# A hand-planned instruction order, computed again with longer transfer prices

## The chip, the cores and the metric

The kernel runs on one core of one Trainium2 chip. The metric is the device time of one execution in microseconds (us); the median of three runs is given, and one further execution was recorded by the profiler.

## The reference

Three layers follow one another. The first is a gated linear recurrence for 4 sequences, 8 heads, 768 steps and heads of 48: per step a complex decay, normalised to at most 0.999 in magnitude, multiplies the 48 x 48 state, the outer product of k and v is added, and q reads the real part. The result is a matrix of 3072 tokens by 384 columns. Two feed-forward layers (384 to 2048 to 384) follow, the first with a leaky ReLU, the second with an ELU:

```
for t in range(S):
    new_re = ar * S_re - ai * S_im
    new_im = ar * S_im + ai * S_re
    S_re, S_im = new_re + k_t v_t^T, new_im
    y[t] = q_t @ S_re
x = reshape(y);  h = x @ w_in;  x = max(0.01 * h, h) @ w_out
h = x @ w_in2;   out = where(h > 0, h, exp(min(h, 0)) - 1) @ w_out2
```

## The kernel before, in words

**Attention.** The 3072 tokens are 24 tiles (6 chunks of 128 steps by 4 sequences). For each tile ScalarE (ACT) and VectorE (DVE) compute decays and phases, scale k and q, and write two halves of `st` (L473, 128 x 768 floats each, cosine and sine part). Each half goes to a scratch tensor in HBM (L480) and is read back with other partitions as `f` (L482); `st` has one buffer. TensorE (PE) transposes `st` (L497), multiplies `f` by `f` (L510) into scores, DVE masks them (`am`, L515), PE multiplies by `v` and by the carried state (L530, L535), and L559 makes the state's increment. The result leaves PSUM in two float16 parts: ACT writes `xh` (L543), and DVE writes the rest, `xl` (L544). Four small moves per tile (L548, two for `xh`, two for `xl`, 12 KB each) then carry rows to other partitions of the same tile.

**Feed-forward.** Three tiles make a block of 384 tokens; there are 8 blocks per layer. A block goes over 16 weight slices: nine hidden matmuls (L596), an activation on ACT and DVE (L604 to L613), and two steps later nine matmuls into accumulators (L632). The blocks' order is written by hand: 1, 1, 2, 1, 2, 1, 2, ... (the layer's number). Weights are loaded as 64-bit words (L326, L329, two raw buffers) and converted to float16 pairs by DVE and ACT (L347 to L359), each slice once before its first use; checks of weights and inputs (L338, L340, L382 and others) fill ACT.

**The planner.** The program doesn't issue these in the order of the code. Every operation is an entry with an engine, a price in ns and its dependences; a transfer is two entries, 475 ns on SP (which issues all transfers, in order) and its own price on one server called DMA, which takes one transfer at a time. `HOPS` gives the delay from one engine's end to another's start: SP to DMA 650, DMA to SP 900. A list scheduler goes forward and backward over the graph for 11 rounds and keeps the order with the earliest end. The engines then run their instructions in that fixed order; real waits are semaphores, so the prices change the order and nothing else, with one exception. Where the plan shows PE idle for more than 700 ns, `(gap - 300) / 220` filler matmuls on the identity are put in (L750, each two records in the trace).

One dependence is known to the program but not to the planner: L544 reads 112 partitions of `xh`, among them rows that the moves of `xh` write. Where a move of `xh` is issued ahead of L544 in the order, L544 waits for it.

Of the kernel before, what the change touches and what calls it, by code (L numbers as in the profile page):

```python
# [124 lines left out]
class Plan:  # L125
# [5 lines left out]
    HOPS = {("DVE", "ACT"): 200.0, ("PE", "ACT"): 200.0, ("PE", "DVE"): 200.0, ("DVE", "PE"): 270.0,  # L131
            ("ACT", "PE"): 270.0, ("PE", "PE"): 0.0, ("ACT", "POOL"): 270.0, ("DVE", "POOL"): 160.0,
            ("DVE", "SP"): 120.0, ("PE", "SP"): 190.0, ("SP", "DMA"): 650.0, ("DMA", "SP"): 900.0,
            ("DMA", "DVE"): 907.0, ("DMA", "ACT"): 908.0, ("DMA", "PE"): 1067.0, ("DMA", "POOL"): 983.0}
    SWITCH = 1300.0
    ISSUE = 475.0
    ROUNDS = 11
# [131 lines left out]
def fast_path(ctx, tc, aa, kq, vt, w_in1, w_out1, w_in2, w_out2, st_dram, out):  # L269
    nc = tc.nc  # L270
# [24 lines left out]
    plan = Plan(lambda table: nc.scalar.preload_act_table_set(sets[table]))  # L295
# [102 lines left out]
    def attention(i):  # L398
# [55 lines left out]
        def scan_t():  # L454
            for j in range(KJ):
# [6 lines left out]
                r=[ph], w=[nf])  # L462
# [14 lines left out]
        scr = st_dram[i % 2]  # L477
        dr = plan.buf(None, None, None, "scr", 2)
        for cs in range(2):
            plan.op("SP", 1150, lambda cs=cs: nc.sync.dma_start(  # L480
                scr[cs].rearrange("(p j) w -> p j w", j=KJ), st.t[:, cs]), r=[st.part(cs)], w=[dr.part(cs)])
            plan.op("SP", 1900, lambda cs=cs: nc.sync.dma_start(  # L482
                f.t[D * cs:D * (cs + 1)], scr[cs].rearrange("(h d) w -> d h w", d=D)), r=[dr.part(cs)], w=[f.part(cs)])
        fp = [f.part(0), f.part(1)]

# [4 lines left out]
        if not last:  # L490
            kn = plan.buf(cp, [P, H, 2, DE, KJ], F32, "kn", KN_BUFS)
            for cs in range(2):
                pt = pa()

                def tr(cs=cs, pt=pt):
# [6 lines left out]
                    r=[pt], w=[kn.part(cs)])  # L502
        am = []
        for g in range(2):
            pt = pa()

            def sc(g=g, pt=pt):
# [9 lines left out]
                r=[pt], w=[m])  # L517
# [27 lines left out]
            xl.t[:wide, :, span], py4(), SX, xh.t[:wide, :, span], ALU.mult, ALU.subtract), r=[py, xh], w=[xl])  # L545
        for z, xz in enumerate((xh, xl)):
            for r in range(2):
                plan.op("SP", 200, lambda xz=xz, r=r: nc.sync.dma_start(  # L548
                    xz.t[64 * r + D:64 * (r + 1), 0:KJ, span],
                    xz.t[64 * r:64 * r + D, KJ, span]),  # L550
                    r=[xz], w=[x1[k][z].part((q, r))])
        parts = [xh, x1[k][0].part((q, 0)), x1[k][0].part((q, 1))]
        squares(parts, lambda: xh.t[:, 0:KJ, span], N, lambda: flags.t[:, 2, i:i + 1], flags.part((2, i)))
        if not last:
# [11 lines left out]
            else:  # L566
                plan.op("DVE", dve(N), lambda: V.tensor_tensor(state[b].t, pk3(), state[b].t, ALU.add),
                        r=[pk], w=[state[b]])
            if c % 2:
# [7 lines left out]
                    r=[rows], w=[pe])  # L577
                plan.op("DVE", dve(N), lambda: V.tensor_tensor(
                    state[b].t, state[b].t, pe.t[:2 * D, :H].unsqueeze(2).to_broadcast([2 * D, H, D]), ALU.mult),
                    r=[pe], w=[state[b]])  # L580
# [86 lines left out]


    running = {i: attention(i) for i in range(NT)}

    def attend(k):
# [267 lines left out]
```

## Time and profile before

| | before |
|---|---|
| median of 3 runs | 997.23 us (995.08 to 998.86) |
| the profiled execution | 991.79 us, of it a span of 990.0 us |
| PE busy | 931.8 us (94%), 6441 matmul records |
| ACT busy, DVE busy | 700.4 us (71%), 677.9 us (68%) |
| transfers | 121.92 MB, 41.1% of 16 engines' span on the SP queue |

PE's records overlap, so its busy share says only where it had something in flight. A window's clock is the mean granted TensorE clock as a share of 2.4 GHz; 0.50 is the lower level, 1.2 GHz. The chain of work that ended last is followed back from the last instruction.

### The profile page before, as it was taken

The numbers are of one execution on the slowest core, as the hardware profiler recorded it, in microseconds if no ns is written. First come the engines' busy times: TensorE is split into PE (matmuls) and PEld (weight loads), VectorE is DVE, ScalarE is ACT, GpSimd is POOL, SyncE is SP. The second block draws the span as 40 slices with busy tenths as digits, with TensorE's granted clock in tenths as the row PEclk, the third lists the DMA queues.
The fourth block names the chain that finished last, engine by engine and source line by source line (L and its number), as shares of the span: only waits on it lengthen the run. The fifth ranks groups of instructions, "written<-read, shape, count | busy, mean of one in ns | idle before, by whom it ended". The sixth has DMA issues, their size and how long they took to land.

```text
span 990.0 us, 17096 instructions
## 1 busy us (share of the span) xinstructions
PE 931.8 (94%) x6441; PEld 616.9 (62%) x6441; DVE 677.9 (68%) x1328; ACT 700.4 (71%) x1526; POOL 1.5 (0%) x21
## 2 busy tenths in 40 slices
PE   4498989999899899999989999999999999999997
PEld 4496666566666657666656667666665666666664
DVE  7878989999786568755677558855587554445553
ACT  6756578676599899999989756875578654345553
POOL 0000000000000000000000000000000000000000
PEclk8697999999899999999999999999999999999999
DMA  7783683664536636935668003620146002000000
GB/s 246 227 241 122 212 230 119 189 201 148 154 118 196 168 99 193 280 116 157 198 163 239 29 11 98 180 63 1 44 116 208 25 1 55 25 1 1 13 13 28
DMA packets 86747, 121.92 MB, mean 123 GB/s; under 512 B 11904, under 2 KB 69248, under 8 KB 86656
## 3 DMA queue, kind: packets, MB, share of 16 engines
q1 hardware_dynamic: 86656, 120.75, 41.1%
q8 instruction: 52, 0.85, 0.4%
q14 instruction: 39, 0.32, 0.1%
HBM read 95.94 MB, written 23.59 MB: 121 GB/s over the span
## 4 chain that ended last, share of the span: by engine, by line
PE 52%; ACT 19%; DVE 16%; DMA 9%; issue 3%; SPq 1%; DVEq 0%; ACTq 0%
PE acc L632 22%; PE h L596 22%; ACT wr L340 3%; DMA wr<-in_w_in 3%; PE pa L510 2%; ACT gh L612 2%; DMA xh<-xh 2%; DMA f<-stack_scratch 2%; DVE st L473 2%; DVE w L359 2%; ACT wt L338 2%; PE h L750 2%; DVE wt L349 2%; DVE g L609 1%; DVE wr L352 1%
## 5 line engine op out<-in xcount | busy, mean ns | idle before, releaser
L596 PEld LDWEIGHTS <-w 128*128 128x128 f16 x2304 | 225.2, 98 | 151.7 <-issue 8.5
L613 DVE TENSOR_TENSOR gl<-g,gh 128x384 f16<-128x384 f32 x256 | 141.5, 553 | 88.7 <-ACT gh L612 84.9
L612 ACT ACTIVATE gh<-g 128x384 f16<-128x384 f32 x256 | 133.2, 521 | 90.9 <-DVE g L609 88.4
L632 PE MATMUL acc<-w,gh 128*128 128x384 f16 x768 | 189.1, 329 | 0.0
L632 PE MATMUL acc<-gh,w 128*128 128x384 f16 x768 | 187.3, 326 | 0.3 <-ACT o L664 0.3
L609 DVE SCALAR_TENSOR_TENSOR g<-h,g 128x384 f32<-128x384 f32 x256 | 141.5, 553 | 54.9 <-ACT g L604 51.0
L632 PEld LDWEIGHTS <-w 128*128 128x128 f16 x1152 | 112.5, 98 | 75.1 <-issue 2.0
L596 PE MATMUL h<-yh,w 128*128 128x384 f16 x768 | 146.5, 327 | 3.2 <-DVE g L609 3.2
L596 PE MATMUL h<-xh,w 128*128 128x384 f16 x768 | 145.7, 326 | 0.5 <-DVE g L609 0.2
L632 PE MATMUL acc<-w,gl 128*128 128x384 f16 x384 | 126.0, 328 | 2.3 <-DVE gl L613 2.3
L632 PE MATMUL acc<-gl,w 128*128 128x384 f16 x384 | 125.2, 326 | 1.4 <-DVE gl L613 1.3
L632 PEld LDWEIGHTS <-gh 128*128 128x128 f16 x768 | 75.0, 99 | 48.7 <-issue 2.3
L608 DVE TENSOR_SCALAR g<-g 128x384 f32<-128x384 f32 x128 | 45.5, 356 | 77.8 <-ACT g L607 77.5
L606 ACT ACTIVATE g<-h 128x384 f32<-128x384 f32 x128 | 62.2, 486 | 49.5 <-PE h L596 47.4
L604 ACT ACTIVATE g<-h 128x384 f32<-128x384 f32 x128 | 62.0, 484 | 32.8 <-PE h L596 32.4
L596 PE MATMUL h<-xl,w 128*128 128x384 f16 x384 | 83.3, 326 | 0.0
L596 PE MATMUL h<-yl,w 128*128 128x384 f16 x384 | 83.3, 326 | 0.0
L607 ACT ACTIVATE g<-g 128x384 f32<-128x384 f32 x128 | 66.6, 521 | 2.4
L340 ACT ACTIVATE wr<-wt,consts 128x768 f32<-128x768 f32 x64 | 64.3, 1005 | 0.4
L632 PEld LDWEIGHTS <-gl 128*128 128x128 f16 x384 | 37.8, 98 | 29.0 <-DVE gl L613 3.9
L510 PE MATMUL pa<-f 96*128 96x128 f32 x384 | 49.7, 282 | 6.3 <-DMA f<-stack_scratch 3.4
L510 PEld LDWEIGHTS pa<-f 96*128 96x128 f32 x384 | 47.8, 197 | 9.2 <-issue 3.3
(99 smaller groups left out, 1121.8 us busy)
## 6 DMA issues: line engine op xcount, KB each, us to landing
wr<-in_w_out SPq DMA_DIRECT2D x64, 384.0 KB, 3.5
wr<-in_w_in SPq DMA_DIRECT2D x64, 384.0 KB, 4.1
stack_scratch<-st SPq DMA_DIRECT2D x48, 384.0 KB, 3.9
f<-stack_scratch SPq DMA_DIRECT2D x48, 384.0 KB, 5.6
kq<-in_kq SPq DMA_DIRECT2D x24, 384.0 KB, 4.8
re<-in_aa SPq DMA_DIRECT2D x32, 192.0 KB, 2.4
im<-in_aa SPq DMA_DIRECT2D x32, 192.0 KB, 2.7
v<-in_v SPq DMA_DIRECT2D x24, 192.0 KB, 3.4
```

The lines of the kernel that those rows point to most:

```text
L338: plan.op("ACT", act(2 * DM), lambda: S_.activation(t.t, raw.t[:, :, :, 1].bitcast(F32), AF.Abs), r=both, w=[t])
L340: plan.op("ACT", act(2 * DM) + 2 * EXTRA, lambda side=side, scale=scale, bias=bias: S_.activation(raw.t[:, :, :, 0].bitcast(F32), t.t, AF. ...
L510: T_.matmul(pt.t[:, hh * C:(hh + 1) * C], lhsT=f.t[:, h, 0:C], rhs=f.t[:, h, C:2 * C], start=True, stop=True)
L596: T_.matmul(ph.t[:, :n], lhsT=w.t[:, 0, z, j * P:(j + 1) * P], rhs=x.t[:, j, :n], start=(m == 0), stop=(m == len(seq) - 1))
L604: plan.op("ACT", act(n, True), lambda: S_.activation(g.t[:, :n], ph.t[:, :n], AF.Copy, scale=0.01 * c), r=[ph], w=[g])
L606: plan.op("ACT", act(n, True), lambda: S_.activation(g.t[:, :n], ph.t[:, :n], AF.Relu, scale=-1.0 / (SX * SW)), r=[ph], w=[g])
L607: plan.op("ACT", act(n), lambda: S_.activation(g.t[:, :n], g.t[:, :n], AF.Exp, scale=-1.0), w=[g], table="L")
L608: plan.op("DVE", dve(n, True), lambda: V.tensor_scalar(g.t[:, :n], g.t[:, :n], -1.0, SG, ALU.add, ALU.mult), w=[g])
L609: plan.op("DVE", dve(n), lambda: V.scalar_tensor_tensor(g.t[:, :n], ph.t[:, :n], c, g.t[:, :n], ALU.mult, ALU.max), r=[ph], w=[g])
L612: plan.op("ACT", act(n), lambda: S_.activation(gh.t[:, :n], g.t[:, :n], AF.Copy), r=[g], w=[gh])
L613: plan.op("DVE", dve(n), lambda: V.tensor_tensor(gl.t[:, :n], g.t[:, :n], gh.t[:, :n], ALU.subtract), r=[g, gh], w=[gl])
L632: T_.matmul(acc[o].t[:, :width], lhsT=pair[0], rhs=pair[1], start=(f == 0 and m == 0), stop=(f == KF - 1 and m == 2))
```

## The change

Eight prices of the planner are raised. No instruction of the program is added, taken away or altered apart from the fillers, whose number follows the plan's gaps.

```diff
-            ("DMA", "DVE"): 907.0, ("DMA", "ACT"): 908.0, ("DMA", "PE"): 1067.0, ("DMA", "POOL"): 983.0}
+            ("DMA", "DVE"): 1400.0, ("DMA", "ACT"): 1400.0, ("DMA", "PE"): 1800.0, ("DMA", "POOL"): 983.0}
...
         for cs in range(2):
-            plan.op("SP", 1150, lambda cs=cs: nc.sync.dma_start(
+            plan.op("SP", 1500, lambda cs=cs: nc.sync.dma_start(
                 scr[cs].rearrange("(p j) w -> p j w", j=KJ), st.t[:, cs]), r=[st.part(cs)], w=[dr.part(cs)])
-            plan.op("SP", 1900, lambda cs=cs: nc.sync.dma_start(
+            plan.op("SP", 2350, lambda cs=cs: nc.sync.dma_start(
                 f.t[D * cs:D * (cs + 1)], scr[cs].rearrange("(h d) w -> d h w", d=D)), r=[dr.part(cs)], w=[f.part(cs)])
...
             for r in range(2):
-                plan.op("SP", 200, lambda xz=xz, r=r: nc.sync.dma_start(
+                plan.op("SP", 600, lambda xz=xz, r=r: nc.sync.dma_start(
                     xz.t[64 * r + D:64 * (r + 1), 0:KJ, span],
```

## Rows read from the trace of the kernel before

**Rows 1.** Windows by stage: us, each engine's busy time, clock, transfer share, GB/s

```profile
0.00:100.00 100.00, 66.44 (x504) 60.75 (x505) 82.34 (x150) 63.73 (x123) 1.54 (x21) 0.81 0.69 210
100.00:250.00 150.00, 144.96 (x1015) 94.39 (x1013) 143.05 (x260) 103.22 (x216) 0.00 (x0) 1.00 0.63 186
250.00:520.00 270.00, 257.89 (x1814) 168.84 (x1814) 181.88 (x375) 246.67 (x550) 0.00 (x0) 0.98 0.56 166
520.00:960.00 440.00, 439.75 (x2975) 279.41 (x2974) 260.42 (x526) 276.33 (x619) 0.00 (x0) 1.00 0.22 63
```

**Rows 2.** Chain of work that ended last, late part: start, us, what

```profile
565.43 1.79 PE pa L510 x16
...
868.60 1.46 PE h L596 x9
...
917.84 2.44 PE acc L632 x15
```

**Rows 3.** The same chain of work, first 92 us

```profile
39.10 9.59 PE h L750 x66
...
66.21 5.67 DMA xh<-xh
...
83.42 6.33 PE h L750 x36
89.75 1.48 PE h L596 x9
```

**Rows 4.** Timeline of SP, 65 to 67 us

```profile
65.73 0.43 SPq L326 DMA_DIRECT2D wr<-in_w_in  x1
```

**Rows 5.** Timeline of PE, 77 us: in brackets idle before, and its releaser

```profile
77.86 1.12 PE L530 MATMUL pa<-am,v 128*64 128x128 f32 x8 [4.68 <-DVE am L515]
```

**Rows 6.** Waits of DVE: us in total, times, longest

```profile
DVE xl L544 <- DMA xh<-xh: 21.3, 9, 5.3
```

**Rows 7.** The chain of work, 254 to 266 us

```profile
254.85 3.72 DMA xh<-xh
...
259.41 2.08 PE pa L510 x8
...
262.45 1.71 PE pa L510 x8
264.16 2.19 PE h L596 x9
```

**Rows 8.** Waits of PE: us in total, times, longest

```profile
PE pa L510 <- DMA f<-stack_scratch: 3.4, 4, 2.6
...
PE pa L510 <- DVE xl L544: 2.0, 1, 2.0
```

**Rows 9.** The chain of work, 487 to 509 us

```profile
487.17 5.00 DMA stack_scratch<-st
493.69 8.71 DMA f<-stack_scratch
...
502.54 2.03 PE pa L510 x16
504.57 4.11 PE acc L632 x15
```

**Rows 10.** Windows of three short stretches, columns as in the first group

```profile
75.00:89.60 14.60, 11.13 (x69) 10.39 (x70) 13.19 (x25) 8.74 (x19) 0.00 (x0) 0.65 0.44 132
261.00:264.20 3.20, 3.20 (x15) 2.64 (x14) 2.37 (x5) 1.52 (x4) 0.00 (x0) 0.50 0.04 9
502.50:507.20 4.70, 4.66 (x25) 3.21 (x26) 2.95 (x7) 3.56 (x9) 0.00 (x0) 0.71 0.45 147
```

**Rows 11.** Transfer issues: KB each, median us from issue to landing

```profile
stack_scratch<-st SPq DMA_DIRECT2D x48, 384.0 KB, 3.9
f<-stack_scratch SPq DMA_DIRECT2D x48, 384.0 KB, 5.6
...
xh<-xh SPq DMA_DIRECT2D x48, 12.0 KB, 1.8
```

## The prediction

> **What bounds the kernel now.** I read the windows by stage first, then the chain of work, then who waits for whom. From 520 to 960 us PE is never idle for more than a quarter of a microsecond, at full clock [rows 1]: no order of the same instructions makes this part shorter. From 100 to 250 us PE is idle for 150 - 144.96 = 5.0 us while DVE is full, and from 250 to 520 us for 270 - 257.89 = 12.1 us while ACT is 91% busy [rows 1]. Ahead of that, the first hidden matmul starts at about 89.6 us [rows 3], and 16 us of the chain before it are filler [rows 3]. So the time is a start-up of some 90 us, then a PE that has work nearly always, then a short tail. An order can win or lose only (a) when the first hidden matmul starts and (b) in the some 17 us of stalls up to 520 us, with what they cost in clock.
>
> Which of these rest on a transfer? Three places do.
>
> First, at 66.21 us a move of `xh` takes 5.67 us, and the chain of work passes through it [rows 3]. It was issued right behind a weight load of 384 KB [rows 4]. `xl` sat behind it, its longest wait of this kind being 5.3 us [rows 6], then the mask, then PE, which was idle for 4.68 us [rows 5]. The clock in the stretch to the first hidden matmul was 0.65 [rows 10], so part of it ran at the lower level of 1.2 GHz.
>
> Second, at 254.85 us another move takes 3.72 us [rows 7]; PE waits 2.0 us for `xl` [rows 8]. Behind the wait the clock is 0.50 [rows 10]: the sixteen records of L510 take 2.08 + 1.71 = 3.79 us where they take 1.79 at full clock, and nine hidden matmuls 2.19 where they take 1.46 [rows 2, 7]. The lower clock costs 2.0 + 0.7 = 2.7 us, the place 4.7 us.
>
> Third, at 493.69 us the read-back of `f` takes 8.71 us [rows 9], and PE waits 2.6 us for it (the whole of this kind is 3.4 us in four waits) [rows 8]. Behind it the clock is 0.71 [rows 10]: fifteen matmuls take 4.11 us against 2.44, L510 2.03 against 1.79 [rows 2, 9], which costs 1.9 us; the place costs 4.5 us.
>
> **The change part by part.** No instruction's own duration changes; PE, DVE and ACT have the same work. What changes is how early the plan thinks data arrives, and so what stands ahead of its user.
>
> *The stack's way out and back.* Issue to use was planned as 475 + 650 + 1150 + 900 = 3.2 us out and 475 + 650 + 1900 + 1067 = 4.1 us back, 7.3 us for one half. It becomes 3.5 and 5.3, 8.8 us: 1.5 us more, and 2.0 us more for the second half, which queues on the planner's one server. The rows' medians to landing alone are 3.9 and 5.6 [rows 11], 9.5 us; the late one took from 487.17 to 502.40, 15.2 us [rows 9]. So both plans are short, the new one less. At the third place some 2.0 us more of other matmuls (a group is 1.46 us [rows 2]) would stand ahead of L510: of the wait of 2.6 us, 0.6 is left, too little, I take it, to bring the clock down. Gain 2.0 + 1.9 = 3.9 us; the other three waits, 0.8 us together, go as well. Bounds: 0 if the read lies elsewhere in the new order and is as late, 5.3 if all of it goes. I take -4.4 (3.9, and 0.5 of the 0.8).
>
> Here a rule of the Trainium skill speaks against the change. The row says 3.9 and 5.6 us for 384 KB [rows 11]. The page "DMA: Bandwidth & Descriptors", section "Anatomy of one DMA", prices a transfer at about 2.0 us fixed plus its bytes over 436 GB/s, an estimate of 2.9 us for this size. By that price the old plan's 3.2 and 4.1 us already covered the transfers, the term would be 0 instead of -4.4, and the sum 4.4 us higher. The trace's durations stand against it.
>
> *The moves.* Their planned price goes from 200 to 600 ns, with the landing at PE from 1067 to 1800. The row has 1.8 us to landing [rows 11]; 475 + 650 + 200 was 1.3 us, and becomes 1.7. PE had no wait that names a move directly. The cost came through L544 behind a move of `xh`, which the planner doesn't see, before or after. What changes is urgency: four moves take 2.4 us of the planner's server instead of 0.8, so the second move of `xh` must go earlier, ahead of loads that can wait, and is less often caught behind 384 KB of weights. If it then takes its median of 1.8 us instead of 5.67, `xl` starts 3.9 us sooner in the start-up, where DVE's order sets the first hidden matmul. Bounds: 0 (caught again) and 5.3 (no wait at all); I take -3.5, a tenth less than 3.9, as DVE's other work is reordered too. The place at 254.85 goes the same way: 0 to -4.7, and as it is one tile of 21 that follow, I take half, -2.4.
>
> *Fillers.* The plan's gaps ahead of transferred data grow, and with them the fillers. Ahead of the first hidden matmul the gap grows by 0.8 us (two moves of one part, 400 ns each) and 0.73 us of landing, 1.5 us: 1500 / 220 makes 6 or 7 more. The 18 fillers there took 6.33 us, 0.35 us each [rows 3], not 0.22, and the hidden matmul came right behind them: fillers and not data set its start. Six more cost 2.1 us. Bounds: 0 if the clock is full and the data later than the fillers; 5.6 if the nine that the stack's 2.0 us add ahead of the first score lie on the path too, (6 + 10) x 0.35. I take +2.1.
>
> *Landing at DVE and ACT.* Loads of weights and inputs are planned as arriving 0.5 us later. They are issued as buffers come free; SP has nothing else to hold them. I take 0, hidden under DVE's 143 of 150 us and ACT's 247 of 270 [rows 1]; without that cover it is 0.5 us per slice of weights that follows another without other work.
>
> *The new order as such.* Every later choice of the scheduler shifts, so new collisions come. The nearest rows are the two places after the start, 4.7 and 4.5 us; between none and two more such, 0 to 9.2, I take +2.0, under half of one.
>
> Sum: -4.4 - 3.5 - 2.4 + 2.1 + 2.0 = -6.2 us against the profiled 991.8 us, so 985.6. That execution lies 5.4 us below the median of 997.2; carried over to the median the forecast is 991.0 us. Ends: -5.3 - 5.3 - 4.7 = -15.3 gives 982; with what the lower clock takes in the start-up ((0.35 - 0.22) x 18 = 2.3 us) 979.6. No gain, and +5.6 + 9.2 = 14.8, gives 1012.
>
> **The rivals.** *The stalls only move.* PE is full for 440 us in a row, and the stalls that rest on a transfer are three; a new order has its own, as likely as dear. Gains and losses cancel, 997 us. For it: 9 waits of `xl` [rows 6] come from a dependence that the change doesn't teach the planner. It also covers the case that only the fillers differ.
>
> *A later start: slower.* `st` has one buffer, so in the plan the next tile's `st` waits for the way out: 0.35 + 0.49 us more, twice ahead of the third tile, 1.7 us. With 2.0 us for the read-back and 1.5 us for the moves the plan starts the first block 5.2 us later, and puts 5.2 / 0.22 = 23 fillers in. At 0.35 us each they take 8.2 us. All behind is PE work without gaps, so a late start is paid in full: 997.2 + 5.2 to 8.2, some 1004 us. Transfers are already busy 69% of the first 100 us [rows 1], so a plan with one server may be pushed. Against it: DVE, 82% busy there, has other work to fill with. It decides the sign when the first hidden matmul starts more than 5 us later than 89.6 and the two later places aren't mended.
>
> **How the numbers follow.** About 0.5%, 5 us, is what a measurement of this kernel can tell from no change: faster means under 992.2, slower over 1002.2. The forecast (waits shrink, 991, own range 980 to 996) gets 0.44; its middle lies near the bound, but the cases in which both moves escape lie well under it, so I put 0.36 of it under and 0.08 in the band. Stalls that only move (997, 988 to 1003) get 0.30: 0.06 under, 0.22 within, 0.02 over. The later start (1004, to 1012) gets 0.26: 0.03 within, 0.23 over. Together 0.42, 0.33 and 0.25. The range of 979 to 1007 takes in the forecast's lower end and most of the late start, and leaves out some 1.5 in 10.
>
> **What would show it.** Right: the first hidden matmul at or before 89 us with a few more fillers ahead of it; PE's waits for `f` under 1 us; no wait of `xl` above 3 us at 60 to 75 and 250 to 260 us; PE's idle time of 250 to 520 us down from 12 to about 6 us. Wrong: a first hidden matmul after 94 us, or the clock under 1.00 in windows after 100 us at new places, or `xl` waiting as long as before.

## The result and the profile after

The changed kernel takes 984.4 us (median of 3 runs, 983.27 to 985.72) against 997.23. The ratio is 0.9874, with a 95% interval of 0.9838 to 0.991: faster, and inside the forecast range of 979 to 1007. Its profiled execution took 983.27 us with a span of 981.5 us, 8.5 us less than the span of before.

The windows by stage of the changed kernel (us, busy time of PE, its weight loads, DVE, ACT and POOL, clock, transfer share, GB/s):

```profile
0.00:100.00 100.00, 68.09 (x564) 61.98 (x565) 86.41 (x160) 67.88 (x132) 1.54 (x21) 0.86 0.75 226
100.00:250.00 150.00, 145.56 (x1054) 96.60 (x1051) 142.24 (x255) 102.83 (x217) 0.00 (x0) 1.00 0.62 183
250.00:520.00 270.00, 259.82 (x1817) 168.56 (x1817) 186.97 (x387) 253.12 (x564) 0.00 (x0) 0.99 0.58 173
520.00:960.00 440.00, 440.00 (x2978) 279.57 (x2976) 256.38 (x514) 271.29 (x602) 0.00 (x0) 1.00 0.19 56
```

Beside [rows 1]: PE is as full after 520 us as before, as it must be. What differs is the first 250 us, in which DVE does 86.41 + 142.24 = 228.7 us of its work where it did 225.4, and the next 270 us, in which PE's idle time falls from 12.1 to 10.2 us and ACT does 253 us of its work instead of 247.

The first layer's hidden matmuls, as the view of one line shows them (duration min/median/max in ns, first and last start in us), of the kernel before and then of the one after:

```profile
L596 PE MATMUL h<-xh,w x768: 322/326/326, 89.6 to 883.4; 128*128 128x384 f16 x192
```

```profile
L596 PE MATMUL h<-xh,w x768: 322/326/328, 88.1 to 875.9; 128*128 128x384 f16 x192
```

So of the 8.5 us, 1.5 come from the earlier first hidden matmul, 6.0 from the stretch between the first and the last of that layer (793.8 to 787.8 us), 1.0 from behind it.

Who waited for whom after the change, PE first and then DVE (us in total, times, longest). Two rows answer to [rows 6, 8]; PE's wait for `g` has grown:

```profile
PE h L596 <- DVE g L609: 9.4, 9, 2.6
...
PE pa L510 <- DMA f<-stack_scratch: 0.3, 1, 0.3
```

```profile
DVE xl L544 <- DMA xh<-xh: 15.9, 7, 3.6
```

Before, the row for `g` was this:

```profile
PE h L596 <- DVE g L609: 3.3, 6, 1.3
```

PE's waits for `f` went from 3.4 to 0.3 us, though the read-back itself is no quicker. The transfer issues after the change (KB each, median us from issue to landing) have it at 6.2 us, against 5.6 in [rows 11]; the moves, too, are slower:

```profile
stack_scratch<-st SPq DMA_DIRECT2D x48, 384.0 KB, 3.5
f<-stack_scratch SPq DMA_DIRECT2D x48, 384.0 KB, 6.2
...
xh<-xh SPq DMA_DIRECT2D x48, 12.0 KB, 2.8
```

The data isn't earlier; its users stand later in PE's order. The tile for which PE waited at 502.5 us with the clock at 0.71 behind it [rows 8, 9, 10] (the 15th in the order) shows it: its second read-back took 8.71 us before and 8.82 after, but between the issue of that read-back and L510, PE's timeline has 21 feed-forward matmuls before and 39 after. L510 now starts 0.87 us after the landing, without a wait for it, and the window behind it has full clock:

```profile
491.81 1.95 PE L510 MATMUL pa<-f 96*128 96x128 f32 x16
```

```profile
491.80:496.50 4.70, 4.49 (x39) 3.35 (x39) 4.70 (x12) 4.70 (x13) 0.00 (x0) 1.00 0.31 92
```

In the start-up, PE's timeline has 23 fillers (two records each) at 0.23 us, not 0.35, right ahead of the first hidden matmul:

```profile
82.92 5.37 PE L750 MATMUL h<-ident 128*128 128x128 f32 x46
88.12 1.14 PE L596 MATMUL h<-xh,w 128*128 128x384 f16 x6
```

The fillers end sooner, the data comes later. SP's timeline has the last two moves of `xl` that the first block needs, before and then after:

```profile
84.56 1.20 SPq L548 DMA_DIRECT2D xl<-xl  x2
```

```profile
86.69 1.20 SPq L548 DMA_DIRECT2D xl<-xl  x2
```

The second one landed at 87.0 us before, and the fillers ran on to 89.6; after the change it landed at 89.1 us, and the part of the nine matmuls that reads `xl` starts at 89.25.

The place at 254 us is not mended. The chain of work after the change runs through two late moves there, and PE's timeline shows what they lead to:

```profile
248.44 6.38 DMA xh<-xh
...
264.12 2.56 DMA xh<-xh
...
266.77 0.69 DVE xl L544
267.47 0.47 DVE g L609
```

```profile
267.98 2.08 PE L596 MATMUL h<-yh,w 128*128 128x384 f16 x6 [2.59 <-DVE g L609]
```

`xl` waits for the move, DVE's next instruction `g` waits behind `xl`, and PE waits 2.59 us for `g`. The view of waits puts this down to DVE; the chain shows the transfer behind it. The window that follows has a clock of 0.69:

```profile
266.00:271.50 5.50, 3.52 (x13) 1.66 (x13) 4.72 (x10) 3.35 (x7) 0.00 (x0) 0.69 0.22 53
```

### The profile page after: what moved, and what is told of

It is laid out like the page before. It is cut to its first block, busy times and chain, and to the rows that moved or that the text cites. A ratio compares the mean times of both kernels' runs of the same rounds, so it can differ in the third digit from the quotient of the medians.

```text
span 981.5 us, 17222 instructions
## 1 busy us (share of the span) xinstructions
PE 928.3 (95%) x6499; PEld 615.4 (63%) x6499; DVE 678.4 (69%) x1328; ACT 701.8 (72%) x1526; POOL 1.5 (0%) x21
## 4 chain that ended last, share of the span: by engine, by line
PE 54%; ACT 19%; DVE 14%; DMA 8%; issue 3%; SPq 1%; DVEq 0%; ACTq 0%
PE h L596 25%; PE acc L632 25%; ACT wr L340 4%; DMA wr<-in_w_in 3%; DMA xh<-xh 2%; ACT gh L612 2%; PE pa L510 2%; DVE w L359 2%; ACT wt L338 2%; DVE gl L613 1%; DVE g L609 1%; DVE wt L349 1%; DVE wr L352 1%; DVE st L473 1%; ACT g L607 1%
## 5 line engine op out<-in xcount | busy, mean ns | idle before, releaser
L596 PE MATMUL h<-yl,w 128*128 128x384 f16 x384 | 83.8, 328 | 0.0
L510 PE MATMUL pa<-f 96*128 96x128 f32 x384 | 47.6, 276 | 0.9 <-issue 0.6
L510 PEld LDWEIGHTS pa<-f 96*128 96x128 f32 x384 | 46.0, 192 | 3.2 <-issue 1.2
```

Of the source, the lines that this page charges most:

```text
L510: T_.matmul(pt.t[:, hh * C:(hh + 1) * C], lhsT=f.t[:, h, 0:C], rhs=f.t[:, h, C:2 * C], start=True, stop=True)
L596: T_.matmul(ph.t[:, :n], lhsT=w.t[:, 0, z, j * P:(j + 1) * P], rhs=x.t[:, j, :n], start=(m == 0), stop=(m == len(seq) - 1))
```

## The experiments

The table has all kernels; ratios are to the kernel before, run beside it on the same chip, with their 95% interval. "First" is the first hidden matmul, "xl" DVE's wait in L544 for a move of `xh`, "f" PE's wait in L510 for the read-back (in e9 and e10 with waits that the view names after a move, see there), "DVE" the busy time of DVE in the first 250 us; all these are of one profiled execution.

| kernel | ratio | first, us | xl, us | f, us | DVE, us |
|---|---|---|---|---|---|
| before | 1 | 89.6 | 21.3 | 3.4 | 225.4 |
| after | 0.9874 (0.9838 to 0.991) | 88.1 | 15.9 | 0.3 | 228.7 |
| e1 landing only | 1.0001 (0.9984 to 1.0019) | 87.3 | 22.1 | 0.4 | 222.8 |
| e2 stack only | 0.9807 (0.9792 to 0.9823) | 83.8 | 8.8 | none | 233.0 |
| e3 moves only | 1.0012 (0.9993 to 1.0031) | 87.2 | 21.9 | 4.6 | 223.5 |
| e4 all lowered | 1.028 (1.0257 to 1.0302) | 85.3 | 36.5 | 8.9 | 208.9 |
| e5 before, shuffled | 1.009 (1.0056 to 1.0123) | 88.2 | 31.6 | 2.7 | 218.2 |
| e6 before, shuffled | 0.9985 (0.996 to 1.0009) | 88.3 | 25.5 | 2.3 | 219.8 |
| e7 stack, shuffled | 0.9783 (0.9745 to 0.9821) | 83.8 | 8.6 | none | 235.6 |
| e8 stack, shuffled | 0.9921 (0.9893 to 0.9948) | 93.2 | 16.2 | 1.1 | 224.9 |
| e9 before, `xl` first | 0.9881 (0.9836 to 0.9925) | 84.1 | 0 | 11.7 | 226.6 |
| e10 after, `xl` first | 0.9741 (0.9697 to 0.9785) | 91.6 | 0 | 0.7 | 237.8 |
| e11 stack, `xl` first | 0.9789 (0.9745 to 0.9833) | 87.5 | 0 | none | 237.5 |
| e12 after, fewer fillers | 0.9912 (0.9883 to 0.994) | 86.4 | 17.6 | 1.3 | 226.9 |

### Which of the prices: e1 to e4

The diff raises six prices, not eight: three landing delays, two prices of the stack's transfers and one of the moves. Three kernels raise one of these groups each, and a fourth lowers all six by about as much. The theories were the forecast's (A: longer prices put more work ahead of late data) and a draw (B: any other order would scatter as much).

e1, the landing delays alone:

```diff
-            ("DMA", "DVE"): 907.0, ("DMA", "ACT"): 908.0, ("DMA", "PE"): 1067.0, ("DMA", "POOL"): 983.0}
+            ("DMA", "DVE"): 1400.0, ("DMA", "ACT"): 1400.0, ("DMA", "PE"): 1800.0, ("DMA", "POOL"): 983.0}
```

> Only the landing delays of data at DVE, ACT and PE are raised (907 to 1400, 908 to 1400, 1067 to 1800); the transfers' own prices stay. Theory A (longer prices put more work ahead of late data): 0.73 us of the 2.0 us more lead that the read-back of f gets, so the wait for f near 500 us shrinks by a third only; about 0.3 to 0.6% faster than before (992 to 994 us). Theory B (the gain is the luck of another order): anywhere between 0.985 and 1.015, with stalls at new places.

Measured: 1.0001. The wait for `f` did go (0.4 us), more than expected, and the time did not. A miss for A as stated: PE's waits for `f` are not by themselves what the gain is made of. DVE's wait in `xl` stayed at 22.1 us and PE had new ones behind it:

```profile
PE pa L497 <- DVE xl L544: 5.3, 2, 4.2
...
PE pa L510 <- DMA f<-stack_scratch: 0.4, 1, 0.4
```

e2, the stack's transfers alone:

```diff
-            plan.op("SP", 1150, lambda cs=cs: nc.sync.dma_start(
+            plan.op("SP", 1500, lambda cs=cs: nc.sync.dma_start(
...
-            plan.op("SP", 1900, lambda cs=cs: nc.sync.dma_start(
+            plan.op("SP", 2350, lambda cs=cs: nc.sync.dma_start(
```

> Only the transfers of the stack are raised (1150 to 1500, 1900 to 2350). Theory A: the read-back of f gets 0.8 to 1.25 us of the 2.0 us, the wait of 2.6 us for f drops below 1.5 us, its clock fall may go; 0.3 to 0.6% faster than before. PE's waits for f below 2 us in all. Theory B: anywhere between 0.985 and 1.015.

Measured: 0.9807, three to six times the expected gain, and better than all six prices together. The first hidden matmul comes at 83.8 us, 5.8 us earlier. DVE does 89.51 us of work in the first 100, where it did 82.34 [rows 1]:

```profile
0.00:100.00 100.00, 70.89 (x573) 63.71 (x574) 89.51 (x164) 69.75 (x136) 1.54 (x21) 0.88 0.81 236
```

e3, the moves alone:

```diff
-                plan.op("SP", 200, lambda xz=xz, r=r: nc.sync.dma_start(
+                plan.op("SP", 600, lambda xz=xz, r=r: nc.sync.dma_start(
```

> Only the moves between partitions are raised (200 to 600). Theory A as forecast: the second move of xh goes earlier than loads, the wait of xl in the start-up goes; 0.3 to 0.5% faster than before, longest wait of xl below 4 us. Against it: in the changed kernel xl still waited 15.9 us in all, so the price may do nothing for it, and the ratio is 0.995 to 1.005. Theory B: anywhere between 0.985 and 1.015.

Measured: 1.0012, with `xl` waiting 21.9 us, the longest of these 5.4 us. The wait of 5.3 us in the start-up did go (the longest ahead of 100 us is 1.2 us), but others of 4.9 and 5.4 us came at 126 and 253 us. So in this order a higher price on the moves does not free `xl`; the alternative written beside the forecast's expectation is the one that came.

e4, all six lowered:

```diff
-            ("DMA", "DVE"): 907.0, ("DMA", "ACT"): 908.0, ("DMA", "PE"): 1067.0, ("DMA", "POOL"): 983.0}
+            ("DMA", "DVE"): 414.0, ("DMA", "ACT"): 416.0, ("DMA", "PE"): 334.0, ("DMA", "POOL"): 983.0}
...
-            plan.op("SP", 1150, lambda cs=cs: nc.sync.dma_start(
+            plan.op("SP", 800, lambda cs=cs: nc.sync.dma_start(
-            plan.op("SP", 1900, lambda cs=cs: nc.sync.dma_start(
+            plan.op("SP", 1450, lambda cs=cs: nc.sync.dma_start(
-                plan.op("SP", 200, lambda xz=xz, r=r: nc.sync.dma_start(
+                plan.op("SP", 50, lambda xz=xz, r=r: nc.sync.dma_start(
```

> All eight prices are lowered by about as much as the change raised them (landing 414, 416, 334; stack 800 and 1450; moves 50). Theory A: data is still later than planned, PE's waits for f grow from 3.4 to over 8 us, each with a clock fall; slower than before by 1% or more (1007 us or over). Theory B: another draw, as likely faster as slower, between 0.985 and 1.015, and not slower for waits on transfers.

Measured: 1.028, as A has it, though not each wait for `f` has a fall of the clock behind it (the one of 1.3 us at 529.5 us has none). The first hidden matmul is earlier than before (85.3 us), and the stretch from it to the last one of that layer is longer, 832.2 us against 793.8. PE's and DVE's waits on transfers, and the window of 100 to 250 us with PE at a clock of 0.94:

```profile
PE pa L510 <- DMA f<-stack_scratch: 8.9, 6, 3.8
```

```profile
DVE xl L544 <- DMA xh<-xh: 36.5, 11, 7.6
```

```profile
100.00:250.00 150.00, 137.70 (x929) 91.06 (x928) 131.20 (x239) 97.18 (x207) 0.00 (x0) 0.94 0.59 166
```

An early first matmul is no gain if the plan behind it counts on data that isn't there. The direction of the prices matters; but how much of 0.9874, or of 0.9807, is the luck of one order, these four can't say.

### How much is the luck of an order: e5 to e8

A price moved by a hair makes the scheduler land on another order: the load of an activation table by 10 ns, or the issue of a transfer on SP by 3 ns. Two such orders with before's prices, two with the stack's prices raised as in e2:

```diff
-    SWITCH = 1300.0
+    SWITCH = 1310.0
```

```diff
-    ISSUE = 475.0
+    ISSUE = 478.0
```

> The prices of before, with one unrelated price moved by a hair (the load of an activation table, 1300 to 1310 ns), so that the scheduler lands on another order with no better knowledge of transfers. Theory A (the stack's price itself helps): such an order is about as good as before, ratio 0.995 to 1.005, and PE's waits for f stay at 3 us or more. Theory B (the gain is a draw among orders): the ratio scatters as the four runs so far did, by more than 1% either way.

> The prices of before with another hair: the issue of a transfer on SP at 478 instead of 475 ns. Theory A: ratio 0.995 to 1.005. Theory B: by more than 1% either way. Both this and the run beside it near 1.00 would bound what the luck of an order is worth; one of them at 0.98 would make the stack's gain doubtful.

> Only the stack's transfers raised, as in the run at 0.981, and the table load at 1310 instead of 1300 ns. Theory A: stays at 0.975 to 0.988, PE's waits for f below 1 us. Theory B: back anywhere between 0.98 and 1.015.

> Only the stack's transfers raised, and the issue of a transfer at 478 instead of 475 ns. Theory A: stays at 0.975 to 0.988, PE's waits for f below 1 us. Theory B: back anywhere between 0.98 and 1.015.

Measured: 1.009 and 0.9985 with before's prices, 0.9783 and 0.9921 with the stack's. With the first order of each, before's prices have 1, 1.009 and 0.9985 (mean 1.0025), the stack's 0.9807, 0.9783 and 0.9921 (mean 0.9837). The two sets don't overlap, and the means differ by 1.9%. The other kernels without a changed edge in the graph fall into place: e1 and e3, with the stack's old price, at 1.0001 and 1.0012, the changed kernel, with the raised one, at 0.9874. That is five orders with the old price at 0.9985 to 1.009, and four with the raised one at 0.9783 to 0.9921: the price of the stack is worth something in every order tried. But within a set the orders lie up to 1.4% apart. That is as much as the change itself brought, so one order's 1.3% can't be split finely: 0.9874 for all six prices beside 0.9807 for two is inside the scatter, and so are e1 and e3 at 1.000. Theory A as written missed the ratios of e5 (0.995 to 1.005) and e8 (0.975 to 0.988), and the waits for `f`, which were 2.7 and 2.3 us in e5 and e6 (3 or more) and 1.1 in e8 (under 1); theory B (no difference between the sets) missed the sets.

Over the kernels so far, `xl`'s wait for a move went with the time: 8.6 and 8.8 us at 0.978 and 0.981, 36.5 us at 1.028. This made a third theory, C: the price matters because `xl` waits less.

### Taking the unplanned wait away: e9 to e11

The planner is told that the moves of `xh` come behind L544. No price is changed; the moves of a tile start behind its L544, which no longer has a move ahead of it, and the scheduler finds another order:

```diff
-                    r=[xz], w=[x1[k][z].part((q, r))])
+                    r=[xh, xl] if z == 0 else [xl], w=[x1[k][z].part((q, r))])
```

> The prices of before; the planner is told that the moves of xh follow L544, so that L544 never waits for them (the program's other dependences stay). Theory C (the time follows L544's unplanned wait for a move of xh: 8.6 to 36.5 us over the ten kernels so far, ratio 0.978 to 1.028): the wait is 0, the ratio 0.97 to 0.985 without any change of price. Theory A (prices alone, through the lead of f): ratio 0.995 or more, as the waits for f stay. The moves themselves start some 0.7 us later in each tile, which costs at most a few us.

> The changed kernel, with the moves of xh told to follow L544. Theory C: the wait of 15.9 us goes to 0 and the ratio from 0.987 to 0.97 to 0.98. Theory A: stays at 0.98 to 0.99, since its waits for f are 0.3 us already.

> Only the stack's prices raised, and the moves of xh told to follow L544. Theory C: little is left of the wait (8.8 us), so 0.970 to 0.980, near the run with after's prices and the same edit. If prices work for themselves too, this is below the run with before's prices by 0.5% or more.

Measured: 0.9881 with before's prices, 0.9741 with after's, 0.9789 with the stack's alone. The wait is gone in all three; DVE's remaining waits at L544 are for ACT.

So the wait is a cost as far as these orders show: without it the kernel before is 1.2% faster, the changed one 1.3% (0.9741 / 0.9874 = 0.9866, from two separate measurements). Each is one order, though, and orders lie up to 1.4% apart: e9 is under all five with the stack's old price, e10 has the lowest ratio of all, but e11 lies among e2, e7 and e8. C in its strong form falls. With no such wait in either, after's prices are still 1.4% faster than before's (0.9741 / 0.9881 = 0.9858), one order each. A straight line through the eleven kernels that have the wait would promise 1.6 us of time per us of wait, 33 us for before's 21.3; taking it away gave 1.2%, 12 us.

Part of the rest went into waits for `f`. In e9, which keeps the short prices, PE waits six times at L510 for the read-back, and the view names three of these waits after a move:

```profile
PE pa L510 <- DMA xh<-xh: 8.2, 3, 2.9
...
PE pa L510 <- DMA f<-stack_scratch: 3.5, 3, 1.9
```

```profile
497.07 3.45 PE L510 MATMUL pa<-f 96*128 96x128 f32 x16 [2.88 <-DMA xh<-xh]
```

By the landing times, all six end 0.14 us after the tile's second read-back has landed; for the three named after a move that is at 128.63, 378.01 and 496.93 us, and no move lands between the read-back and L510. So PE waits 11.7 us for `f`, where it waited 3.4 before, and behind the three longest of these waits the clock was 0.50 or 0.51 for 3.4 to 6.9 us. (This execution took 987.32 us, 5.4 more than the kernel's median.) So in e9, where `xl` is no longer late but the price of the stack is short, PE gets to the read-back ahead of the data. In e10, with the raised prices, the first row is 0.7 us and the second isn't there; a further wait of 0.8 us that the view puts down to "issue" ends with a read-back too. e10 is the best kernel of the study, 967.5 us in the median, 2.6% under before. From 100 to 250 us its PE is never idle and DVE does 148.66 of 150 us; before it was 143.05 [rows 1]:

```profile
100.00:250.00 150.00, 150.00 (x1096) 101.31 (x1094) 148.66 (x271) 108.62 (x229) 0.00 (x0) 1.00 0.63 188
```

### Fillers: e12

The same order as the changed kernel's, with fewer fillers in the same gaps:

```diff
-                idle[n] = int((gap - 300.0) / 220.0)
+                idle[n] = int((gap - 300.0) / 350.0)
```

> The changed kernel in the same order, with 350 instead of 220 ns per filler, so about 107 fillers instead of 172. Forecast's filler term (fillers set the start of the first hidden matmul, at 88.1 us right behind 23 of them): the start comes 1 to 3 us sooner and the ratio falls from 0.987 to 0.984 to 0.986. Rival: data sets that start, or PE falls to the lower clock without them: 0.987 or more.

Measured: 0.9912. The first hidden matmul does start 1.7 us sooner, at 86.39 us, but its `xl` part then waits for the move, and starts at 88.95 us where it started at 89.25. The gain is 0.3 us:

```profile
86.39 1.14 PE L596 MATMUL h<-xh,w 128*128 128x384 f16 x6
88.95 0.65 PE L596 MATMUL h<-xl,w 128*128 128x384 f16 x3 [1.41 <-DMA xl<-xl]
```

Some 5 us later a wait of 1.60 us for `g`, which the changed kernel has as well (1.59 us), is followed by matmuls at the lower clock here, six in 2.02 us instead of 1.14, and not there:

```profile
94.23 2.02 PE L596 MATMUL h<-xh,w 128*128 128x384 f16 x6 [1.60 <-DVE g L609]
```

The clock of 100 to 250 us is 0.97 instead of 1.00. The fillers cost the changed kernel nothing that can be seen; the rival written beside the forecast's filler term is the one that came. Whether they earn the 0.4% between 0.9912 and 0.9874 stays open: the intervals overlap, and the trace of e12 is of an execution 3.5 us above its median.

## Why the prediction was right, point by point

**What bounds the kernel.** Right: after 520 us nothing moved, and the gain came from ahead of it. But the start of the first hidden matmul decides less than forecast: it is at 91.6 us in e10, which has the lowest ratio, and at 85.3 in e4, which has the highest. A better measure is how much of its work DVE has done by 250 us; before, DVE was busy for 82% of the first 100 us and 95% of the next 150, PE for 66% and 97% [rows 1]. Over the fourteen kernels of the table the time goes with it: 208.9 us at 1.028, 225.4 at 1, 228.7 at 0.9874, 233 to 238 at 0.974 to 0.981. It is no strict rule (224.9 at 0.9921), and only a reading of the table: it says how far the work has got, not why, and no run changes DVE's share alone.

**The stack's way out and back (-4.4 us).** The mechanism is the one forecast, more work ahead of a read that is as late as ever: 39 feed-forward matmuls in place of 21 at the third place, waits of 3.4 us that became 0.3 (under 1 us even with one of 0.6 us that the view puts down to "issue" and that ends with a read-back), and no fall of the clock behind the long one. The price of the Trainium skill ("DMA: Bandwidth & Descriptors", "Anatomy of one DMA") gives an estimate of 2.9 us for 384 KB, by which the old prices were long enough. The page fits it to transfers that GpSimd issues; here SP issues them, among other traffic, the medians after are 3.5 and 6.2 us, and e2, which raises only these two prices, gains 1.9%. The size was off. As e1 loses the waits for `f` and gains nothing, and e2 gains far more than 4.4 us, the stack's price does more than give the read-back its lead. In e2's profiled execution, 5.8 us come from the earlier first hidden matmul and 9.6 from the stretch to the last one of that layer. In this stretch PE's idle time is 14.9 us instead of 18.1, and the 10.2 us at the lower clock that the kernel before has there (258.7 to 265.5 and 504.4 to 507.8 us) are gone; at half speed those are worth an estimated 5.1 us. The traces of e7, e8 and e10 have no time at the lower clock there either; e4 has 30.7 us. Why the start-up is shorter (the spacing of transfers on the planner's one server, or the order of DVE's work that follows from it) is not separated by these runs.

**The moves (-3.5 and -2.4 us).** Here a step failed: "the second move of `xh` must go earlier ... and is less often caught behind 384 KB of weights". e3, which raises this price alone, has `xl` waiting 21.9 us where it was 21.3, at other places, and no gain. In the changed kernel the start-up's wait of `xl` did fall from 5.3 to 2.1 us, near the forecast 3.5, but with e3 at 1.0012 this is not shown to be worth anything by itself, and the last moves of `xl` ahead of the first hidden matmul landed 2.1 us later, not earlier; at 250 to 270 us `xl` is caught twice, and PE pays with a wait of 2.59 us and a clock of 0.69. What takes the wait away is an edge in the planner's graph (e9 to e11), not a price.

**Fillers (+2.1 us).** Ahead of the first hidden matmul 23 came in place of 18, five more where six or seven were forecast (172 in place of 143 in the whole kernel), and they cost nothing: at full clock the 23 took 5.37 us, what the plan allows for them, and the data came no earlier (e12). That is the forecast's own lower bound, "0 if the clock is full and the data later than the fillers". Before, the reading was right: the fillers ran 2.6 us past the data. The price of 0.35 us was read from a stretch with a mean clock of 0.64 (83.4 to 89.8 us), behind the late move of the start-up, and doesn't hold where the clock is full. (The term's upper bound of 5.6 us counts ten fillers where its sentence has nine, 5.3 us; and 23 fillers at 0.35 us are 8.1 us, not 8.2. Neither matters for the range.)

**Landing at DVE and ACT (0).** e1 gives 1.0001 with it and with the landing at PE; a gain or loss below the scatter of orders is not excluded.

**The new order as such (+2.0 us).** Undersized in range: beside the first order of their prices, e5 is 0.9% slower and e6 0.2% faster, e8 1.1% slower and e7 0.2% faster. Another order can cost some 11 us, and can also gain a little.

**The sum.** -6.2 us were forecast on the profiled execution and 8.5 measured between the two profiles; between the medians it is 12.8. The term that held is the stack's. The start-up's total, -3.5 + 2.1 = -1.4 against 1.5 measured, is luck: neither part came as reasoned. The data came 2.1 us later, and the gain is that the fillers no longer run past it, as they did by 2.6 us before. Of the 6.0 us between the first and last hidden matmul, 1.2 are idle time of PE (18.1 to 16.9 us), 0.7 are fillers at 93 us that went, and the time at the lower clock fell from 10.2 to 3.4 us (267.8 to 271.2), at half speed an estimated 3.4 us. The long wait for `f` went, but PE's waits for `g` grew from 3.3 to 9.4 us. The middle place, forecast at -2.4, still has its wait, and the lower clock behind it for 3.4 us instead of 6.8. Of the signs named ahead, the first hidden matmul before 89 us and the waits for `f` under 1 us came; `xl` still waited 3.2 us at 254.9 us, and PE's idle time of 250 to 520 us is 10.2 us, not 6. How close the total came is in part the luck of this order: with the stack's prices raised in the same way, other orders gave 0.9783 to 0.9921. Of the rivals, "the stalls only move" describes e1 and e3, the later start describes e8, whose first hidden matmul comes at 93.2 us: it is the slowest of the three orders with the stack's prices, at 0.9921 still ahead of before. That a late start "is paid in full" fails in e10, which starts 2.0 us later than before and has the lowest ratio.

## What to carry to other kernels

Where the order of instructions is fixed ahead of time, price a transfer at what it takes under this kernel's own traffic: here a price too short was paid as a stall on an engine in order, and behind some of these stalls again in TensorE's clock, and all six prices lowered cost 2.8%. Whether prices of the stack's transfers above the measured times would do harm, no run here shows. Judge such a change by several orders, not by one, for a price moved by a hair shifted the time by up to 1.4% here. Then look for waits that the program has and the plan lacks: one edge in the graph was worth about as much as all six prices, and in the one order tried came on top of them.

## What the runs showed that was not expected

A move of 12 KB between partitions, 1.8 us in the median of the kernel before [rows 11], took 5.67 us behind a load of 384 KB [rows 3, 4], and 6.38 us after the change. Some waits of PE of two to three us were followed by the lower clock: 2.0 us for `xl` by 0.50, 2.6 us for `f` by 0.71 [rows 8, 10], 2.59 us for `g` by 0.69 after the change. Others were not: behind a wait of 3.1 us at 247.5 us in e2, and one of 2.8 us at 219.2 us in e9, the clock was 1.00. A wait of 1.6 us for `g` at 92 to 94 us had the lower clock behind it in e12, which had fewer fillers ahead of it, and not in the changed kernel; these are two executions, and the cause is only argued.
